# One ring of six slots, two longer output-weight loads, and 64 contraction rows of a modulation term by a second queue

## The chip, the core and the metric

The kernel runs on one core of a Trainium2 chip. The metric is the device time of one execution in microseconds. TensorE is PE in the profile, VectorE DVE, ScalarE ACT, GpSimd POOL, SyncE SP; SPq and ACTq are the queues on which those engines issue transfers.

## The reference

For a batch of 4 rows, one token each, width 512: six modulation rows come from a conditioning vector, grouped-query attention (32 query heads, 8 key/value heads, a cache of 4096 positions) is added to the residual with a gate, and a token-mixing MLP follows with its own shift, scale and gate. All is fp32.

```python
mod = (silu(c) @ w_mod).reshape(4, 6, 1, 512)          # w_mod: 512 x 3072
sa, ca, ga, sb, cb, gb = (mod[:, i] for i in range(6))
h = layernorm(x) * (1 + ca) + sa
q = (h @ wq)                                            # 512 x 4096
p = softmax(q k^T * 128**-0.5);  o = p v                # 32 caches of k and of v, 2 MB each
x = x + ga * (o @ wo)                                   # wo: 4096 x 512
h = layernorm(x) * (1 + cb) + sb
x = x + gb * (gelu(h * w1 + b1) @ w2 + b2)
```

The inputs weigh 157 MB, of which the key and value caches are 134 MB.

## The kernel before

There are 32 streams (4 batch rows x 8 key/value heads). Stream i has a key tile K[i] and a value tile V[i], each 128 partitions x 16 KB. All loads are issued by SyncE, in the order of the program, on one queue; SyncE waits at an instruction until the place that a load writes is free, and what stands behind it waits too. Below, K3V1 is the load of 4 MB that brings K[3] and V[1].

A pool `ring` holds three buffers of 2 x 16 KB a partition. They take first the modulation weights of terms 0 and 1 (`wm01`), and the two halves of `wq`, then `kk` (K0 and K1), then the pairs K2V0, K3V1, K4V2 and so on. The output weights have buffers of their own, four loads of 2 MB (`load_wo`). The modulation weights of terms 2, 3 and 4 (`wm24`, 3 MB in two loads) take one ring buffer for a while, and term 5 comes last of all.

The order of the instructions is that of the code: the schedule is manual. After the projection of the queries, iteration i of the main loop does for PE: `scores(i+2)` (L231), `pick(i-1)` (L328), `sums(i+1)`, `project(i-1)` (L343), `turn_max(i+2)`, the first half of `values(i)` (L291), `spread_max`, the second half of `values(i)`. So iteration 1 needs K3V1, and iteration 2 needs K4V2. In iteration 2 the three calls `mod(2)`, `mod(3)`, `mod(4)` follow: each multiplies silu(c), held by contraction block k = 0..3, with the four blocks of 128 rows of its weights (L215, tile `pm`), copies the result on ScalarE (L218) and folds the four groups (L221, tile `pc`), and a copy into `prep` frees the PSUM buffer for the next one. The last eight streams follow a written list of steps (`PLAN`), and after the last value tile comes a tail of vector and scalar work that ends in the stores.

Of the kernel before, what the change touches and what calls it, by code (L numbers as in the profile page):

```python
# [20 lines left out]
NSM = 3 * NF + 16 + 1  # L21
# [7 lines left out]
def adaln_decode(ctx: ExitStack, tc: tile.TileContext, small, x, wmod, wq, kk, kv, vv, wo, out):  # L29
# [18 lines left out]
    wm01 = ring.tile([P, 2, 4, D], F32, name="wm01", tag="kv")  # L48
    nc.sync.dma_start(wm01, wmod[0])
# [3 lines left out]
    for k in range(0, 4, 2):  # L53
        t = ring.tile([P, 2, HQ * DH], F32, name=f"wq{k}", tag="kv")
        nc.sync.dma_start(t, wq[k // 2])
        wqt += [t[:, 0], t[:, 1]]
    w1, b1, w2 = sm[:, 0:NF], sm[:, NF:2 * NF], sm[:, 2 * NF:3 * NF]
    cT = sm[:, 3 * NF:3 * NF + 16]
    b2 = sm[:, 3 * NF + 16:]
# [31 lines left out]
    wo_p = [wos.tile([P, 2, REP, D], F32, name=f"wo{h}") for h in range(0, HKV, 2)]  # L91
    wo_t = [wo_p[h // 2][:, h % 2] for h in range(HKV)]
    prep = cst.tile([P, 4, P], F32, name="prep")
    osb = cst.tile([P, B, P], F32, name="osb")
    sT8 = cst.tile([P, 4, B, 8], F32, name="sT8")

    def root(ve, n=P, y=None):
        if y is None:
# [4 lines left out]
    sg = cst.tile([P, 16], F32, name="sg")  # L103
# [3 lines left out]
    sT = cst.tile([P, 4, B], F32, name="sT")  # L107
    dv.tensor_mul(sT.rearrange("p k b -> p (k b)"), sg, cT)  # L108
    nc.gpsimd.tensor_copy(sT8.rearrange("p k b r -> p (k b) r"),
                   sT.rearrange("p k b -> p (k b)").unsqueeze(2).to_broadcast([P, 16, 8]))  # L110
# [46 lines left out]
    KT, VT, WM = {}, {}, {}  # L157

    def slots():
        return ring.tile([P, 2, SK], F32, name="kv", tag="kv")  # L160

    def key(t, i):
        KT[i] = t

    def value(t, i):
        VT[i] = t.rearrange("p (j d) -> p j d", d=DH)

    def load_first():
        t = slots()
        nc.sync.dma_start(t, kk)  # L170
        key(t[:, 0], 0)
        key(t[:, 1], 1)

    def load_pair(i):
        t = slots()
        nc.sync.dma_start(t, kv[i])
        key(t[:, 0], i + 2)
        value(t[:, 1], i)

    def load_wo(h):  # L180
        nc.sync.dma_start(wo_p[h // 2], wo[h // 2])

    def load_wm24():
        w = ring.tile([P, 3, 4, D], F32, name="wm24", tag="kv")
        nc.sync.dma_start(w[:, 0:2], wmod[1])
        nc.sync.dma_start(w[:, 2], wmod[2][:, 0])
        for e in range(3):
            WM[2 + e] = w[:, e]

    def load_wm5():  # L190
        t = slots().rearrange("p s (k n) -> p (s k) n", n=D)
        nc.sync.dma_start(t[:, 0:4], wmod[2][:, 1])
        WM[5] = t[:, 0:4]
        return t[:, 4:6]

    def load_key(t, i):
        nc.sync.dma_start(t, kv[i - 2][:, 0])
        key(t, i)

    def load_v(t, i, cuts):  # L200
        value(t, i)
        src = (kv[i][:, 1] if i < NS - 2 else vv[i - NS + 2]).rearrange("p (j d) -> p j d", d=DH)
        for lo, hi in zip(cuts, cuts[1:]):
            nc.sync.dma_start(VT[i][:, lo:hi], src[:, lo:hi])
# [7 lines left out]
    def mod(t):  # L212
        pm = ps_e.tile([P, D], F32, name=f"pm{t}", tag="e")
        for k in range(4):
            mm(pm[32 * k:32 * k + 32, :], sT8[:, k].rearrange("p b r -> p (b r)"), WM[t][:, k, :],  # L215
               start=True, stop=True)
        yw = wk.tile([P, D], F32, name="ym", tag="yw", bufs=1)
        nc.scalar.activation(yw, pm, AF.Copy)  # L218
        pc = ps_e.tile([P, P], F32, name=f"pc{t}", tag="e")
        for c in range(4):  # L220
            mm(pc[32 * c:32 * c + 32, :], g32, yw[:, c * P:(c + 1) * P], start=True, stop=True)  # L221
        return pc
# [3 lines left out]
    def scores(i):  # L226
        b, h = divmod(i, HKV)
        S[i] = s = ps_s.tile([P, 1024], F32, name=f"s{i}", tag="s")
        for n in range(2):
            for c in range(4):  # L230
                mm(s[32 * c:32 * c + 32, n * 512:(n + 1) * 512], QT[:, b, h, :],  # L231
                   KT[i][:, (n * 4 + c) * 512:(n * 4 + c + 1) * 512], start=True, stop=True)

# [51 lines left out]
    def values(i, ks):  # L285
        if ks[0] == 0:
            PV[i] = ps_v.tile([P, 4 * DH], F32, name="pv", tag="pv")
        pT = PL[i][0]
        for k in ks:
            q = k % 4  # L290
            mm(PV[i][32 * q:32 * q + 32, :], pT[:, 128 * k:128 * k + 128:4],  # L291
               VT[i][:, 4 * k:4 * k + 4, :].rearrange("p j d -> p (j d)"), start=(k < 4), stop=(k >= 4))

    def values_narrow(i, ks, pv=None):
        if ks[0] == 0:
            PV[i] = ps_v.tile([P, DH], F32, name="pvn", tag="pv") if pv is None else pv
        pv = PV[i]
        pT = PL[i][0].rearrange("p (k r) -> p k r", r=32)
        top = 32 if i < NS - 1 else 30
        for k in ks:  # L300
            for j in range(4 * k, min(4 * k + 4, top)):
                c = j % 4
                mm(pv[32 * c:32 * c + 32, :], pT[:, j, :], VT[i][:, j, :], start=(k == 0), stop=(j + 4 >= top))  # L303

# [32 lines left out]
    def project(i, pa=None, between=None):  # L337
        b, h = divmod(i, HKV)
        oT = OT[i]
        if pa is None:  # L340
            pa = ps_m.tile([P, D], F32, name="pa", tag="m")
            for g in range(REP):
                mm(pa[32 * g:32 * g + 32, :], oT[:, g:g + 1].to_broadcast([P, 32]), wo_t[h][:, g, :],  # L343
                   start=True, stop=True)
        else:
            for g in range(REP):
                for c in range(4):
                    mm(pa[32 * c:32 * c + 32, :], oT[:, g:g + 1].to_broadcast([P, 32]),  # L348
                       wo_t[h][:, g, c * P:(c + 1) * P], start=(g == 0 and h == HKV - 2),
                       stop=(g == REP - 1 and h == HKV - 1))  # L350
                if between and g == 1:
                    between()
        PA[i] = pa
# [198 lines left out]
    def finish(b, pg, py, hb, wr):  # L552
        uu = ring.tile([P, 16, D], F32, name="uu", tag="kv")
# [35 lines left out]
    def fold_gate(gate, es):  # L589
        for e in es:  # L590
            w = wo_t[HKV - 2 + e // REP][:, e % REP]
            dv.tensor_tensor_reduce(w, w, gate, 1.0, 0.0, OP.mult, OP.add, rowsum[:, e:e + 1])
# [16 lines left out]
    load_first()  # L609
    load_pair(0)  # L610
    load_wo(0)
    for i in range(2):
        for step in (scores, row_max, turn_max, col_max, spread_max, copy_max, expo):
            step(i)
    for step in (turn, sums, scale):
        step(0)
    mix = None
    for i in range(NS - HKV):
        load_pair(i + 1)
        if i in (1, 3, 5):  # L620
            load_wo(i + 1)
        if i == 1:
            load_wm24()
# [25 lines left out]
        if i == 2:  # L649
            for t in range(2, 5):  # L650
                pm = mod(t)
                dst = prep[:, {2: 1, 3: 2, 4: 3}[t]]
                if t == 4:
                    dv.tensor_scalar(dst, pm, 1.0, None, op0=OP.add)
                else:
                    nc.scalar.activation(dst, pm, AF.Copy)
        if i == NS - HKV - 2:
            gate = spread_gate()
# [4 lines left out]
    pve = pgx = pc = ep = spare = slot = None  # L663
    gates = list(range(2 * REP))
    cuts = {NS - 1: (0, 16, 24, 28, 30, 32), NS - 2: (0, 16, 32)}
    last, halves = [(0, 1, 2, 3), (4, 5), (6,), (7,)], [(0, 1), (2, 3), (4, 5), (6, 7)]
    PLAN = """
    a23 v24.0 A23 p23 t25.0 P23 F R v24.1 LP25 G s26 t25.1 M H V24 LP26 Q a24 S26 v25.0 N s27 x A24 f p24 g
    x LP27 m26 S27 P24 m27 X26 X27 b26 B26 e26 x b27 v25.1 c g t26.1 l25 t26.0 B27 s28 V25 c g L25
    v26.0 v26.1 S28 x l26 f a25 L26 V26 A25 x m28 p25 LT X28 e27 c a26 P25 t27.0 A26 b28 s29 f B28 p26 e28  # L670
    LK30 t27.1 S29 P26 v27.0 m29 l27 g LK31 T t28.1 X29 LT t28.0 s30 L27 S30 b29 v27.1 B29 e29 l28 m30 V27
    LV28 L28 a27 g X30 t29.1 t29.0 l29 L29 s31 A27 LV29 b30 p27 x B30 S31 c c m31 e30 P27 X31 v28.0 f LT LV30
    b31 v28.1 B31 f e31 LV31 l30 V28 L30 t30.1 l31 L31 a28 t31.1 A28 p28 v29.0 v29.1 t30.0 f P28 V29 v30.0 a29
    v30.1 A29 LW p29 f v30.2 v30.3 t31.0 P29 g V30 Y y a30 A30 p30 E x v31.0 f v31.1 v31.2 v31.3 V31 z31 a31 I A31 j p31
# [3 lines left out]
             "l": sums, "L": scale, "V": copy_v, "a": pick, "A": copy_o, "P": add_up,  # L678
             "LP": load_pair}
# [4 lines left out]
    for step in PLAN.split():  # L684
# [19 lines left out]
        elif op == "LT":  # L704
            slot = slots()
        elif op == "LK":
            load_key(slot[:, i % 2], i)
        elif op == "LV":
            load_v(slot[:, i % 2], i, cuts.get(i, (0, 32)))
        elif op == "LW":  # L710
            spare = load_wm5()
        elif op == "x":
            mix.expand(spare if mix.n == 6 else None)
# [75 lines left out]
```

## Time and profile before

| | |
|---|---|
| time, median of 3 runs | 386.42 us (386.37 to 386.49) |
| span of the profiled execution | 384.7 us |
| busy: PE, DVE, ACT, POOL | 298.7, 198.2, 112.2, 7.7 us |
| mean granted TensorE clock | 0.883 |
| read from HBM | 157.32 MB |

The page tells the span of the profiled execution, from its first to its last instruction; no separate time of that execution is given, and the median of the runs lies 1.7 us above the span. In the lines of the chain, a row has the start, the length and what the time went to; in a timeline, start, length, engine, source line, operation, tiles and count, and in brackets the idle time before it with what ended it. One matmul of the code is two records in the trace, so that x8 is four matmuls. A table of windows has for each window the busy time of each engine, the granted clock (1.00 is full speed), the busy share of the 16 DMA engines and GB/s.

### The profile page before, as it was taken

How to read it: one execution, taken by the hardware profiler on the slowest of the kernel's cores; microseconds unless marked ns; L12 is line 12 of the kernel's file. 1: busy time of each engine (PE TensorE's matmuls, PEld its weight loads, DVE VectorE, ACT ScalarE, POOL GpSimd, SP SyncE). 2: the span in 40 equal slices, each digit the busy share in tenths (PEclk: the TensorE clock that was granted, in tenths of full speed). 3: DMA queues.
4: the chain of work that ended last, by engine and by line, in shares of the span. 5: the costliest groups of instructions: out<-in, count | busy, mean ns of one | idle time of the engine just before them, and what ended most of it. 6: DMA issues, size and time to landing. Idle time of an engine off the chain costs nothing.

```text
span 384.7 us, 5604 instructions
## 1 busy us (share of the span) xinstructions
PE 298.7 (78%) x2380; PEld 117.2 (30%) x2380; DVE 198.2 (52%) x407; ACT 112.2 (29%) x144; POOL 7.7 (2%) x33
## 2 busy tenths in 40 slices
PE   0856777866966949979877878788888887999984
PEld 0112122311323313334322222342222343333653
DVE  1130251620451424664866545557665567778757
ACT  1001111121110110212567311124575105657276
POOL 1100000000000000000000000000000000000000
PEclk9989555985695685998999998999999999999999
DMA  8999999999999999999999999999999999999930
GB/s 331 433 433 436 411 453 433 409 432 436 423 441 433 434 436 436 434 436 431 429 425 433 428 433 434 429 433 431 429 434 436 434 436 432 424 417 423 418 122 3
DMA packets 7409, 157.69 MB, mean 410 GB/s; under 512 B 964, under 2 KB 1236, under 8 KB 1496
## 3 DMA queue, kind: packets, MB, share of 16 engines
q1 hardware_dynamic: 7376, 157.33, 95.4%
q8 instruction: 18, 0.29, 0.3%
q14 instruction: 7, 0.06, 0.0%
q10 hardware_dynamic: 8, 0.00, 0.0%
HBM read 157.32 MB, written 0.01 MB: 409 GB/s over the span
## 4 chain that ended last, share of the span: by engine, by line
DMA 60%; PE 29%; DVE 7%; ACT 2%; issue 1%; POOL 0%; SPq 0%; POOLq 0%; DVEq 0%
DMA kv<-in_kv 58%; PE s L231 8%; PE pv L291 7%; PE s L122 2%; PE qs L138 2%; DVE m L236 2%; DVE p L267 2%; DMA sm<-in_small 2%; PE pa L343 2%; PE pt L328 2%; ACT uu L562 1%; PE pb L251 1%; PE pve L303 1%; PE pm L240 1%; PE pgx L348 1%
## 5 line engine op out<-in xcount | busy, mean ns | idle before, releaser
L231 PE MATMUL s<-kv,QT 128*32 128x512 f32 x512 | 75.2, 714 | 38.9 <-DMA kv<-in_kv 37.0
L236 DVE TENSOR_REDUCE m<-s 128x1 f32<-128x1024 f32 x32 | 39.2, 1224 | 96.0 <-PE s L231 95.9
L261 ACT ACTIVATE p<-s,nm 128x1024 f32<-128x1024 f32 x32 | 35.7, 1115 | 180.6 <-DVE nm L256 180.5
L291 PE MATMUL pv<-kv,p 128*32 128x512 f32 x464 | 69.8, 670 | 0.7 <-DMA kv<-in_kv 0.7
L231 PEld LDWEIGHTS s<-kv,QT 128*32 128x32 f32 x512 | 15.8, 123 | 84.0 <-DMA kv<-in_kv 52.5
L328 PEld LDWEIGHTS pt<-g,po 128*128 128x128 f32 x236 | 31.1, 205 | 27.2 <-issue 19.9
L343 PE MATMUL pa<-wo,oT 128*32 128x512 f32 x240 | 34.6, 648 | 4.6 <-DVE oT L335 4.4
L328 PE MATMUL pt<-g,po 128*128 128x4 f32 (+2 forms) x236 | 33.9, 267 | 1.5 <-DVE po L314 1.0
L267 DVE STREAM_TRANSPOSE p<-p 128x1024 f32<-128x1024 f32 x25 | 30.9, 1234 | 0.0
L314 DVE COPY po<-pv 128x512 f32<-128x512 f32 x29 | 20.0, 688 | 16.8 <-PE pv L291 16.7
L245 DVE TENSOR_REDUCE mx<-pm 1x128 f32<-1x512 f32 x32 | 21.3, 669 | 1.1 <-PE pm L240 1.1
L442 DVE TENSOR_SCALAR u<-hb,wr,sm 128x512 f32<-128x512 f32 x40 | 19.9, 541 | 1.9 <-POOL wr L437 1.0
L506 ACT ACTIVATE u<-u 128x1024 f32<-128x1024 f32 x20 | 20.4, 1051 | 1.5 <-DVE u L442 1.4
L361 DVE TENSOR_TENSOR acc<-acc,pa 128x512 f32<-128x512 f32 x26 | 17.8, 686 | 4.3 <-PE pa L343 4.2
L261 ACT ACT_TABLE_LOAD x11 | 14.1, 1283 | 20.3 <-DVE nm L256 20.2
L251 PEld LDWEIGHTS pb<-neg,mx 1*128 1x128 f32 x64 | 10.4, 202 | 28.2 <-DVE mx L245 26.5
L122 PE MATMUL s<-wm,sT 128*4 128x512 f32 x16 | 9.1, 732 | 10.6 <-DVE sT L108 10.6
L506 ACT ACT_TABLE_LOAD x13 | 16.7, 1283 | 0.2
L291 PEld LDWEIGHTS pv<-kv,p 128*32 128x32 f32 x464 | 13.4, 146 | 7.2 <-issue 3.1
L240 PE MATMUL pm<-ident,m 128*1 128x128 f32 x32 | 9.3, 289 | 7.4 <-DVE m L236 3.5
L251 PE MATMUL pb<-neg,mx 1*128 1x1 f32 x64 | 13.1, 271 | 2.1 <-DVE mx L245 2.1
L453 PE MATMUL py<-u,sm 128*32 128x512 f32 x80 | 14.4, 616 | 0.0
(158 smaller groups left out, 214.7 us busy)
## 6 DMA issues: line engine op xcount, KB each, us to landing
kv<-in_kv SPq DMA_DIRECT2D x28, 4096.0 KB, 21.9
wq<-in_wq SPq DMA_DIRECT2D x2, 4096.0 KB, 16.3
wo<-in_wo SPq DMA_DIRECT2D x4, 2048.0 KB
kv<-in_kv SPq DMA_DIRECT2D x4, 2048.0 KB, 20.3
wm<-in_wmod SPq DMA_DIRECT2D x2, 2048.0 KB, 14.8
kv<-in_kk SPq DMA_DIRECT2D x1, 4096.0 KB
kv<-in_vv SPq DMA_DIRECT2D x3, 1024.0 KB
wm<-in_wmod SPq DMA_DIRECT2D x1, 1024.0 KB
```

Of the source, the lines that this page charges most:

```text
L231: mm(s[32 * c:32 * c + 32, n * 512:(n + 1) * 512], QT[:, b, h, :], KT[i][:, (n * 4 + c) * 512:(n * 4 + c + 1) * 512], start=True, stop=True)
L236: dv.tensor_reduce(M[i], S[i], axis=AX.X, op=OP.max)
L245: dv.tensor_reduce(mx, M[i].rearrange("o (c r) -> o r c", c=4).unsqueeze(1).to_broadcast([1, 4, 32, 4]), axis=AX.X, op=OP.max)
L251: mm(pb, M[i].rearrange("o c r -> o (c r)"), neg1, start=True, stop=True)
L261: nc.scalar.activation(p, S[i], AF.Exp, bias=M.pop(i), accum_out=l)
L267: dv.transpose(PL[i][0], PL[i][0])
L291: mm(PV[i][32 * q:32 * q + 32, :], pT[:, 128 * k:128 * k + 128:4], VT[i][:, 4 * k:4 * k + 4, :].rearrange("p j d -> p (j d)"), start=(k < ...
L314: dv.tensor_copy(PV[i], pv)
L328: mm(pt, po[:, c * DH:(c + 1) * DH], sel.unsqueeze(1).to_broadcast([P, m, REP]), start=(c == 0), stop=(c == n - 1))
L343: mm(pa[32 * g:32 * g + 32, :], oT[:, g:g + 1].to_broadcast([P, 32]), wo_t[h][:, g, :], start=True, stop=True)
L442: dv.tensor_scalar(u[:, e, :], hb, wr[:, j:j + 1], b1[:, j:j + 1], op0=OP.mult, op1=OP.add)
L506: nc.scalar.activation(u, u, AF.Gelu_apprx_tanh)
```

## The change

- The pool of three buffers becomes one tile `RING` of six slots of 16 KB a partition. A list `LOADS` holds all loads in the order in which they are issued, and `advance(name)` is called after the last reader of a tile in the code; it issues the loads at the head of the list as far as the slots that they take have been read, and stops at the first that has to be held back.
- `wm01` no longer takes ring space. It is loaded into the place of output weights 0 and 1; `kk` so takes the free slots 4 and 5 at once.
- The output weights come in two loads of 4 MB in place of four of 2 MB. The first goes behind K2V0. The second takes the place in which the weights of terms 2, 3 and 4 lie in the meantime (`wm24` and `low`, inside output weights 4 to 7), so that it is held until `mod(4)` has read them (`advance("M2")`). It stands in the list behind K4V2 and ahead of K5V3.
- The weights of terms 2, 3 and 4 are loaded behind K3V1, 22 KB a partition in one load, and half a block (`wm24[0:64, 11]`) in another. The three `mod` calls move from the end of iteration 2 to the end of iteration 1.
- The last 64 contraction rows of term 3 are brought by ScalarE's queue, in two loads of 8 rows of 8 KB, to 16 of 64 partitions of `low`, which GpSimd sets to zero before. The matching rows of silu(c) come as extra columns of `small`, zeros elsewhere; `mod(3)` uses one matmul over 64 partitions and four more over `low` in place of its fourth.
- In the last eight streams, loads go by slot in place of by pairs of slots.

```diff
-    ring = ctx.enter_context(tc.tile_pool(name="ring", bufs=3))
+    ring = ctx.enter_context(tc.tile_pool(name="ring", bufs=1))
...
-    wm01 = ring.tile([P, 2, 4, D], F32, name="wm01", tag="kv")
-    nc.sync.dma_start(wm01, wmod[0])
+    RING = ring.tile([P, 6, SK], F32, name="kv")
+    wo_t = wos.tile([P, HKV, REP, D], F32, name="wo")
+    wm01 = wo_t[:, 0:2]
+    wm24 = wo_t[:, 4:7].rearrange("p h g n -> p (h g) n")
+    low = wo_t[0:64, 7]
+    nc.sync.dma_start(wm01, wm0)
...
+    nc.gpsimd.memset(low, 0.0)
...
+    def queue():
+        q = [entry(["K0", "K1"], kk)]
+        for i in range(NS - 4):
+            q.append(entry([f"K{i + 2}", f"V{i}"], kv[i]))
...
+        q.insert(2, ("wo", "M0", wo_t[:, 0:4], wo[0]))
+        q.insert(4, ("wo", None, wm24[:, 0:11], wm2))
+        q.insert(5, ("wo", None, wm24[0:64, 11], wm3))
+        q.insert(7, ("wo", "M2", wo_t[:, 4:8], wo[1]))
+        return q
...
+    def advance(name=None):
+        read.add(name)
+        while LOADS:
+            kind, names, *rest = LOADS[0]
+            if kind == "wo":
+                if names not in read:
+                    return
+                nc.sync.dma_start(*rest)
+            else:
+                n, p = len(names), at[0]
+                if any(h not in read for h in held[p:p + n]):
+                    return
...
     def mod(t):
...
-            mm(pm[32 * k:32 * k + 32, :], sT8[:, k].rearrange("p b r -> p (b r)"), WM[t][:, k, :],
-               start=True, stop=True)
+            if t == 3 and k == 3:
+                mm(pm[96:128, :], sT8[0:64, 3].rearrange("p b r -> p (b r)"), wm24[0:64, 11], start=True, stop=False)
+                for q in range(4):
+                    mm(pm[96:128, :], sT8[0:64, 4 + q].rearrange("p b r -> p (b r)"), low[:, q],
+                       start=False, stop=(q == 3))
+            else:
+                mm(pm[32 * k:32 * k + 32, :], sT8[:, k].rearrange("p b r -> p (b r)"), WM[t][:, k, :],
+                   start=True, stop=True)
...
     for i in range(2):
         for step in (scores, row_max, turn_max, col_max, spread_max, copy_max, expo):
             step(i)
+        nc.scalar.dma_start(low[i:64:8].rearrange("p g n -> p (g n)"), wlow[i])
...
     for i in range(NS - HKV):
-        load_pair(i + 1)
-        if i in (1, 3, 5):
-            load_wo(i + 1)
-        if i == 1:
-            load_wm24()
         scores(i + 2)
...
-        if i == 2:
+        if i == 1:
             for t in range(2, 5):
                 pm = mod(t)
...
+            advance("M2")
```

SyncE's queue, from the first key load to the seventh pair, before. `wo` is a load of output weights, `wm` the modulation weights of terms 2 to 4, `kv` a pair, and 128x8192 fp32 elements are 4 MB.

```order
L170 DMA kv<-in_kk 128x8192
L176 DMA kv<-in_kv 128x8192
L181 DMA wo_128<-in_wo 128x4096
L176 DMA kv<-in_kv 128x8192 x2
L181 DMA wo_129<-in_wo 128x4096
L185 DMA wm_337<-in_wmod 128x4096
L186 DMA wm_337<-in_wmod 128x2048
L176 DMA kv<-in_kv 128x8192 x2
```

The same stretch of SyncE's queue in the changed kernel.

```order
L208 DMA kv<-in_kk 128x8192
L208 DMA kv<-in_kv 128x8192
L190 DMA wo<-in_wo 128x8192
L208 DMA kv<-in_kv 128x8192
L190 DMA wo<-in_wm 128x5632
L190 DMA wo<-in_wm 64x512
L208 DMA kv<-in_kv 128x8192
L190 DMA wo<-in_wo 128x8192
L208 DMA kv<-in_kv 128x8192 x25
```

The first `wo` now has twice the bytes and stands ahead of K3V1 as before; the `wm` loads moved from behind K4V2 to ahead of it; and the second `wo` (which waits for `mod(4)`) stands between K4V2 and the 25 pairs from K5V3 on.

TensorE from the scores of iteration 2 through the modulation terms, before (`s` scores, `pt` pick, `pa` project, `pv` values, `pm_445` to `pc_478` the three `mod` calls).

```order
L231 MATMUL s_394<-kv,QT 32x512 x8
L328 MATMUL pt<-g_122,po 128x4 x4
L275 MATMUL pl<-g_122,l 128x4
L343 MATMUL pa<-wo_128,oT 32x512 x4
L240 MATMUL pm<-ident,m 1x128
L291 MATMUL pv<-kv,p 32x512 x4
...
L215 MATMUL pm_445<-wm_337,sT_134 32x512 x4
L221 MATMUL pc_452<-ym,g_122 32x128 x4
L215 MATMUL pm_458<-wm_337,sT_134 32x512 x4
L221 MATMUL pc_465<-ym,g_122 32x128 x4
L215 MATMUL pm_471<-wm_337,sT_134 32x512 x4
L221 MATMUL pc_478<-ym,g_122 32x128 x4
```

TensorE in the changed kernel, from the scores of iteration 1 (`s_332`, which read K3) to those of iteration 2 (`s_430`).

```order
L249 MATMUL s_332<-kv,QT 32x512 x8
...
L366 MATMUL pa<-wo,oT 32x512 x4
...
L310 MATMUL pv<-kv,p 32x512 x4
L233 MATMUL pm_384<-wo,sT_129 32x512 x4
L239 MATMUL pc_391<-ym,g_121 32x128 x4
L233 MATMUL pm_397<-wo,sT_129 32x512 x3
L228 MATMUL pm_397<-wo,sT_129 32x512
L230 MATMUL pm_397<-wo,sT_129 32x512 x4
L239 MATMUL pc_408<-ym,g_121 32x128 x4
L233 MATMUL pm_414<-wo,sT_129 32x512 x4
L239 MATMUL pc_421<-ym,g_121 32x128 x4
L249 MATMUL s_430<-kv,QT 32x512 x8
```

The three terms now stand one iteration earlier, ahead of the scores of iteration 2, and the middle one has eight matmuls in place of four.

More of the change, by code (lines that the diff above doesn't have):

```diff
@@ L180, in load_wo @@
[L180 to L204, printed above, removed]
+    KT, VT, WM = {}, {}, {t: wm24[:, k:k + 4] for t, k in ((2, 0), (3, 4), (4, 7))}
+    held, read = [("Q", 0), ("Q", 0), ("Q", 1), ("Q", 1), None, None], {None, ("Q", 0), ("Q", 1)}
@@ new lines, in adaln_decode, with entry @@
+    cuts = {NS - 1: (0, 16, 24, 28, 30, 32), NS - 2: (0, 16, 32)}
+    def entry(names, src):
+        return ("ring", names, src)
+    def queue():
+        q = [entry(["K0", "K1"], kk)]
+        for i in range(NS - 4):
+            q.append(entry([f"K{i + 2}", f"V{i}"], kv[i]))
+        for i in (NS - 2, NS - 1):
+            q.append(entry([f"K{i}"], kv[i - 2][:, 0]))
+        for i in range(NS - 4, NS):
+            q.append(entry([f"V{i}"], kv[i][:, 1] if i < NS - 2 else vv[i - NS + 2]))
+        q.append(entry(["W5"], wm5))
+        q.insert(2, ("wo", "M0", wo_t[:, 0:4], wo[0]))
[3 more added lines that the diff above has]
+        return q
@@ new lines, in adaln_decode @@
+    LOADS, at = queue(), [4]
+    def advance(name=None):
[10 more added lines that the diff above has]
+                    return
+                for k, nm in enumerate(names):
+                    t, i = RING[:, p + k], int(nm[1:])
+                    if nm[0] == "K":
+                        KT[i] = t
+                    elif nm[0] == "V":
+                        VT[i] = t.rearrange("p (j d) -> p j d", d=DH)
+                    else:
+                        WM[i] = t.rearrange("p (k n) -> p k n", n=D)[:, 0:4]
+                held[p:p + n] = names
+                at[0] = (p + n) % 6
+                if names[0] == "W5":
+                    nc.sync.dma_start(WM[5], rest[0])
+                elif len(names) > 1:
+                    nc.sync.dma_start(RING[:, p:p + n], rest[0])
+                elif names[0][0] == "K":
+                    nc.sync.dma_start(RING[:, p], rest[0])
+                else:
+                    cs = cuts.get(i, (0, 32))
+                    v = rest[0].rearrange("p (j d) -> p j d", d=DH)
+                    for lo, hi in zip(cs, cs[1:]):
+                        nc.sync.dma_start(VT[i][:, lo:hi], v[:, lo:hi])
+            LOADS.pop(0)
@@ L348, in project @@
                     mm(pa[32 * c:32 * c + 32, :], oT[:, g:g + 1].to_broadcast([P, 32]),
-                       wo_t[h][:, g, c * P:(c + 1) * P], start=(g == 0 and h == HKV - 2),
+                       wo_t[:, h, g, c * P:(c + 1) * P], start=(g == 0 and h == HKV - 2),
                        stop=(g == REP - 1 and h == HKV - 1))
@@ L764 @@
     cT = a["c"].reshape(B, 4, P).transpose(2, 1, 0).reshape(P, 16)
+    low = _np.zeros((P, 16), _np.float32)
+    low[0:64].reshape(8, 8, 4, B)[:, 0:2] = a["c"][:, 448:].reshape(B, 8, 2, 4).transpose(1, 2, 3, 0)
+    cT = _np.concatenate([cT, low], axis=1)
     small = _np.concatenate([
```

95 lines of the change are left out of this document (37 added, 58 removed).

## The prediction

> **What bounds the kernel now.** I read the page first (busy time, the DMA lines, the chain's shares), then the chain in order of time, SyncE's queue in the timeline, and last the windows.
>
> ```profile
> span 384.7 us, 5604 instructions
> PE 298.7 (78%) x2380; PEld 117.2 (30%) x2380; DVE 198.2 (52%) x407; ACT 112.2 (29%) x144; POOL 7.7 (2%) x33
> GB/s 331 433 433 436 411 453 433 409 432 436 423 441 433 434 436 436 434 436 431 429 425 433 428 433 434 429 433 431 429 434 436 434 436 432 424 417 423 418 122 3
> q1 hardware_dynamic: 7376, 157.33, 95.4%
> DMA 60%; PE 29%; DVE 7%; ACT 2%; issue 1%; POOL 0%; SPq 0%; POOLq 0%; DVEq 0%
> kv<-in_kv SPq DMA_DIRECT2D x28, 4096.0 KB, 21.9
> ...
> 0.00:2.00 2.00, 0.00 (x0) 0.00 (x0) 0.49 (x2) 1.28 (x1) 0.71 (x7) 1.00 0.56 106
> 0.00:5.00 5.00, 0.00 (x0) 0.00 (x0) 1.42 (x3) 1.28 (x1) 0.71 (x7) 1.00 0.65 206
> 2.00:82.00 80.00, 52.84 (x283) 15.64 (x283) 24.27 (x49) 7.93 (x18) 2.31 (x15) 0.81 0.99 425
> 83.30:362.00 278.70, 229.14 (x1735) 90.57 (x1735) 158.28 (x315) 90.20 (x109) 3.96 (x9) 0.90 1.00 431
> ```
>
> The loads are the bound: from 2 to 362 us the DMA engines are 99 to 100% busy, at 433 GB/s in most slices. A pair of 4.19 MB takes 4.19/0.433 = 9.7 us, but 21.9 us from issue to landing: some 12 us of other loads lie ahead of it when it is issued. As long as that reserve is above zero, waits of SyncE cost nothing. Once it is used up, every microsecond without a load comes back at the end, since the same bytes are still to come:
>
> ```profile
> 63.14 3.30 PE s L231 x16
> ...
> 71.80 22.74 DMA kv<-in_kv
> 94.58 3.64 PE s L231 x16
> ...
> 327.22 15.81 DMA kv<-in_kv
> 343.04 0.14 issue
> ```
>
> The chain runs on loads up to 343.04 us, where K30 has come, and what follows goes with the last tiles. So I ask of each part whether it takes DMA time away, and whether it lets the queue run dry.
>
> **Parts that cost nothing, or little.** `kk` is issued some 17 us sooner, behind loads that are busy anyway (share 0.99 above): 0. The finer releases of the last tiles: 0, by the same reserve. Longer rows of the output weights, 32 KB against 16 KB: the slices in which most tiles of the end are loaded by half (424, 417 and 423, from the 35th on) against those of whole pairs (425 to 436) are slower by 3% at the most, and 8.4 MB take 19 us, so between 0 and -0.6 us; those slices hold still shorter pieces too, so I take -0.1. The 64 rows: 128 KB come by another queue. Spread evenly nothing changes. If an 8-row load runs on 8 of the 16 engines, those carry 16 KB more and all carry 8 KB less; at 433/16 = 27 GB/s an engine that is 0.3 us more or less on the half that ends last, so -0.3 to +0.3, taken 0. ("How many engines" in the Trainium skill's DMA: Bandwidth & Descriptors, section "Why a DMA increments its semaphore by 16 and not by 1", has such a load on the lowest-numbered 8; by it the sum would shift by one of these two ends, and no view here names the engines.)
>
> The zeros for `low` stand on POOL ahead of the sigmoid from which the whole start follows:
>
> ```profile
> 0.74 0.20 POOL masks.py:197 MEMSET ident<- 128x128 f32 x1
> 9.72 0.10 POOL L81 MEMSET eps<- 128x1 f32 x1
> ...
> 50.76 1.11 ACT L261 ACTIVATE p<-s,nm 128x1024 f32<-128x1024 f32 x1 [5.44 <-DVE nm L256]
> ...
> 35.64 0.42 PE L153 MATMUL px<-xr,rows 4*32 4x128 f32 x8
> 37.90 2.94 PE L231 MATMUL s<-kv,QT 128*32 128x512 f32 x16 [1.84 <-DMA kv<-in_kk]
> ...
> 30.10 0.33 SPq L176 DMA_DIRECT2D kv<-in_kv  x1
> 33.53 14.31 SPq L176 DMA_DIRECT2D kv<-in_kv  x2
> ```
>
> 0.10 us for 127 more elements makes 1.6 us for 2048 (an estimate). The query projection is that much later; PE's wait of 1.84 us for `kk` hides it, and the issue of K2V0, at 31.7 in place of 30.10, still comes with `kk` in flight (landing near 37). 0. Without that cover it would be 1.6 us of PE in iteration 0, which has the next wait to spend. The two issues on ACT (0.33 us each, as SP's) fall into its idle time beside the first exponentials (5.44 us before the second): 0.
>
> **The part that costs: the second output-weight load.** It waits for the last matmul of `mod(4)`, and K5V3 and all that follows is queued behind it on SyncE, though K5V3's slots are free long before. Four times decide.
>
> *When the queue runs dry.* Ahead of it stand wm01 2.10, small and x 0.04, wq 8.39, kk, K2V0, K3V1 and K4V2 4.19 each, the first output weights 4.19, the terms 3.15: 34.6 MB, the same bytes as before. The windows moved 0.21 MB to 2 us and 425 x 80 = 34.0 MB to 82 us; the other 0.43 MB make 83.0, and since a packet counts where it starts, I take 83.2. From the other side: K5V3, issued at 71.80 with the queue full, is there for PE at 94.58, less 9.7 is 84.9, which holds the slowest engine and the signal. 83.2 is nearer to the mean over the engines.
>
> *When iteration 1 starts.* K3V1 now has 2.10 MB more ahead of it, 4.84 us: 63.14 + 4.84 = 67.98.
>
> *How long it takes, and the terms behind it.*
>
> ```profile
> 62.60:65.90 3.30, 2.76 (x16) 0.59 (x16) 0.00 (x0) 0.00 (x0) 0.00 (x0) 0.50 0.87 377
> 66.00:83.00 17.00, 12.70 (x102) 4.88 (x98) 9.21 (x16) 2.41 (x4) 0.00 (x0) 1.00 1.00 427
> 83.10:103.50 20.40, 15.63 (x91) 4.32 (x83) 4.01 (x7) 2.35 (x5) 0.00 (x0) 0.50 0.98 424
> 141.20:154.60 13.40, 11.35 (x53) 4.15 (x57) 4.04 (x7) 0.63 (x1) 0.00 (x0) 0.50 1.01 435
> 155.00:160.00 5.00, 4.63 (x43) 2.00 (x39) 3.70 (x6) 0.17 (x2) 0.00 (x0) 1.00 0.97 416
> ...
> 63.14 3.30 PE L231 MATMUL s<-kv,QT 128*32 128x512 f32 x16 [2.54 <-DMA kv<-in_kv]
> 70.64 1.09 PE L291 MATMUL pv<-kv,p 128*32 128x512 f32 x8
> 72.81 1.92 PE L231 MATMUL s<-kv,QT 128*32 128x512 f32 x16 [1.08 <-DMA kv<-in_kv]
> 78.92 1.09 PE L291 MATMUL pv<-kv,p 128*32 128x512 f32 x8
> ...
> 143.25 3.64 PE L231 MATMUL s<-kv,QT 128*32 128x512 f32 x16 [5.20 <-DMA kv<-in_kv]
> 153.61 1.59 PE L291 MATMUL pv<-kv,p 128*32 128x512 f32 x8
> ...
> 82.51 1.47 PE L215 MATMUL pm<-wm,sT 128*32 128x512 f32 x8 [2.49 <-DMA wm<-in_wmod]
> 84.67 0.66 PE L221 MATMUL pc<-ym,g 128*32 128x128 f32 x8 [0.70 <-ACT ym L218]
> 85.73 1.94 PE L215 MATMUL pm<-wm,sT 128*32 128x512 f32 x8 [0.40 <-ACT prep L656]
> 88.44 0.66 PE L221 MATMUL pc<-ym,g 128*32 128x128 f32 x8 [0.78 <-ACT ym L218]
> ```
>
> An iteration depends on the granted clock. After a wait of 2.54 us, iteration 1 of before got the full clock from 66.0 and took 63.14 to 71.73, 8.6 us. One that starts after 5.20 us of waiting stayed at half clock for 13.4 us: 143.25 to 155.20, 11.95 us. One wholly at full clock took 72.81 to 80.01, 7.2 us. In the changed kernel PE waits for K3V1 from 60.6 to 67.98, 7.4 us, and the changes of clock lie on a grid of 3.41 us (66.0 to 83.0 is five, 83.1 to 103.5 six): the scores of before filled the window 62.6 to 65.9 to 2.76 of 3.30 us, and it rose. From 67.98 they would straddle 69.4, 1.4 us and 2.2 us, as those at 143.25 did. I take 11.95: iteration 1 ends at 79.9.
>
> The terms at full clock: pm 1.09 (as `pv`, the same shape), 0.70 for the copy, pc 0.4 (as `px`, 128 columns at full clock), 0.40 for the second copy, 2.6 us; `mod(3)` with twice the matmuls 2.18 + 1.5 = 3.7; pm of `mod(4)` 1.09; together 7.4 us. At half clock: 3.8 + (3.88 + 1.84) + 1.94 = 11.4. Since the iteration that began at 143.25 had the full clock by 155, some 11.5 us after its start, this one has it from about 79.5, and I take 7.4: the last read is at 87.3. The weights are there by then: they follow K3V1 by 3.15 MB, 7.3 us.
>
> *How long until data flows.* The first load is issued at 0.72 and 206 x 5 = 1.03 MB have gone by 5.0 us, which at 433 GB/s began at 2.62: 1.9 us after the issue.
>
> ```profile
> 0.72 0.39 SPq L49 DMA_DIRECT2D wm<-in_wmod  x1
> ```
>
> So the stream resumes at 89.2 where it ended at 83.2: 6.0 us without loads. Nothing later gives them back: after it the wo load, K5V3 and K6V4 stand in the queue at once (29 us), while iteration 2 (some 88 to 100) frees the slots of K7V5. The terms leave iteration 2, but there they lay in PE's wait for K5V3 (81 to 94.5 us): no gain.
>
> **The sum**, on the profiled execution: 384.7 + 6.0 - 0.1 = 390.6, and with the 1.7 us around it 392.3; on the median 386.4 + 5.9 = 392.3.
>
> **Rivals.**
>
> *Iteration 1 gets the full clock early.* Then it ends at 67.98 + 8.6 = 76.6, the last read is at 84.0, data at 85.9, 2.7 us dry: 389.0. For it: the scores are dense, 3.6 us at half clock, and fill one window if it starts near them. Against it: the longer wait, and the grid as it lay in this execution. The Trainium skill's TensorE: Matmul & The Clock Gate ("What's actually happening") calls the window of 4096 cycles free-running, not reset by the kernel's start; the 3.41 us grid agrees, and by that rule the phase could be another in each run.
>
> *The terms stay at half clock.* 79.9 + 11.4 = 91.3, data at 93.2, 10 us dry: 396.4. For it: all three ran so at 83 to 92 us, with gaps for the copies. Against it: the window ahead of them is full of `pv`.
>
> *The queue does not run dry (not slower).* The second wo load has to be issued ahead of 83.2 - 1.9 = 81.3. With the fastest rows, 67.98 + 7.2 + 7.4 = 82.6, it misses that by 1.3 us; it decides if K3V1 comes sooner, or a warm queue takes a new load in less than 1.9 us. Then only the rest of the sum is left: 386.4 - 0.1, with the balance of the engines at best -0.4: 386.0 to 386.6. A gain above 0.2% would need both of those ends and something I don't see.
>
> **How the numbers follow.** Half-clock iteration with full-clock terms, as summed, 0.47 (390.7 to 394, its ends being the dry time 84.9 and part of the terms at half clock); full clock early 0.27; terms at half clock 0.12; never dry 0.10, of which nearly all ends within 0.2% (0.8 us; the runs before lay within 0.12 us of each other); faster by another way 0.04. The likeliest gives 392.3. The range, 388.4 to 396.5, takes in the first three cases with half of the third's spread. Slower 0.87, same 0.09, faster 0.04.
>
> **What would show it.** In the slices of the page, GB/s falls to some 300 in the ninth and tenth (77 to 96 us), where it was 432 and 436; on SyncE a wait of its wo issue on PE `pm` L233, with the issue near 87; PE `s` of iteration 1 at 68 with a DMA wait of about 7 us; the later slices as before, and the chain's end later by the hole. If the hole is missing and the time still rises, the start (POOL's zeros) or the tail is at fault. The prediction fails if the clock is granted sooner at 68 to 80 us, or if a queue that has just emptied restarts faster than at the kernel's start.

## The result, and the profile after

The changed kernel takes 395.78 us (median of 5 runs, 395.02 to 396.04) against 386.49 us before (5 runs, 386.37 to 387.85): a ratio of 1.0233, 95% interval 1.0219 to 1.0247, so 9.3 us slower where 5.9 were predicted. The profiled execution took 395.8 us with a span of 394.0, which is 9.3 us over the span of before.

The page after has the hole where it was forecast, deeper than forecast. Rows: span; busy time; GB/s in 40 slices of 9.85 us; the queue of the 8-row loads, with packets and MB; the chain's shares.

```profile
span 394.0 us, 5617 instructions
PE 294.9 (75%) x2388; PEld 116.7 (30%) x2388; DVE 198.4 (50%) x407; ACT 112.2 (28%) x144; POOL 9.6 (2%) x34
GB/s 327 429 429 452 394 419 427 404 238 314 426 427 426 434 442 436 434 429 427 426 428 439 437 433 431 432 429 424 432 431 449 427 434 427 422 423 428 415 118 4
q10 hardware_dynamic: 40, 0.13, 0.1%
DMA 59%; PE 30%; DVE 6%; ACT 2%; issue 1%; POOL 1%; SPq 0%; POOLq 0%; DVEq 0%; ACTq 0%
```

POOL is busy for 9.6 us in place of 7.7, the zeros. The ninth and tenth slices moved 238 and 314 GB/s. The fifth and eighth, 394 and 404, are a little lower than those of before (411 and 409, in slices of 9.62 us): around the two 8-row loads, which ScalarE issues near 43 and 47 us, and the half block. Slices that begin at other times compare only roughly. Windows of the same microseconds (length; PE, PEld, DVE, ACT, POOL busy; granted clock; DMA share; GB/s) make this sharper. After:

```profile
44.00:56.00 12.00, 7.61 (x36) 2.08 (x32) 6.29 (x9) 1.20 (x2) 0.00 (x0) 0.64 1.03 410
72.00:77.00 5.00, 5.00 (x27) 2.71 (x27) 3.08 (x5) 0.00 (x0) 0.00 (x0) 0.50 1.02 363
77.00:84.00 7.00, 5.89 (x43) 1.35 (x36) 1.66 (x4) 2.08 (x4) 0.00 (x0) 0.93 1.01 433
84.00:92.20 8.20, 6.28 (x45) 1.66 (x47) 0.29 (x1) 1.47 (x3) 0.00 (x0) 1.00 0.28 88
92.20:362.00 269.80, 215.73 (x1599) 84.56 (x1588) 155.18 (x301) 84.47 (x101) 3.95 (x9) 0.92 1.00 431
```

Two of the same windows of before:

```profile
44.00:56.00 12.00, 9.06 (x40) 2.62 (x35) 4.67 (x8) 2.41 (x4) 0.00 (x0) 0.50 1.01 434
72.00:77.00 5.00, 3.98 (x34) 1.76 (x34) 2.69 (x4) 0.21 (x2) 0.00 (x0) 1.00 1.02 433
```

So there are two losses. From 84 to 92.2 us the queue is nearly empty (share 0.28), and at 44 to 56 and 72 to 77 us the engines are fully busy (1.03 and 1.02) but move only 410 and 363 GB/s. From 92.2 to the end the rate is as before, and nothing comes back.

The chain after, in order of time (start, length, what), and SyncE's timeline and wait:

```profile
35.28 33.40 DMA kv<-in_kv
...
79.70 0.90 PE pm L233 x8
...
84.13 3.45 PE pm L230 x8
...
89.13 1.11 PE pm L233 x8
90.29 0.33 SPq L190
90.62 0.05 issue
90.67 22.20 DMA kv<-in_kv
```

```profile
90.29 0.33 SPq L190 DMA_DIRECT2D wo<-in_wo  x1
90.67 234.52 SPq L208 DMA_DIRECT2D kv<-in_kv  x25
...
SPq L190 <- PE pm L233: 13.4, 1, 13.4
```

In front of the second output-weight load SyncE first waits 32.0 us for the weights of the terms to land, and then 13.4 us for the last `pm` of `mod(4)`, which reads them; all 25 pairs stand behind it. The three terms in TensorE's timeline:

```profile
68.73 3.64 PE L249 MATMUL s<-kv,QT 128*32 128x512 f32 x16 [10.67 <-DMA kv<-in_kv]
...
82.10 1.06 PE L233 MATMUL pm<-wo,sT 128*32 128x512 f32 x6 [0.40 <-ACT prep L673]
83.09 1.04 PE L228 MATMUL pm<-wo,sT 64*32 64x512 f32 x2
83.97 3.59 PE L230 MATMUL pm<-wo,sT 64*32 64x512 f32 x8
89.13 1.06 PE L233 MATMUL pm<-wo,sT 128*32 128x512 f32 x8 [0.40 <-ACT prep L673]
```

Eight records of `pm` take 1.06 us when they go to four groups of 32 columns (the last row), and the four matmuls over `low` take 3.59 us at the same full clock: all four write `pm[96:128]`, one group, and run one behind another.

### The profile page after: what moved, and what is told of

It reads as the page before. It is cut to its first block, busy times and chain, and to the rows that moved or that the text cites. A ratio compares the mean times of both kernels' runs of the same rounds, so it can differ in the third digit from the quotient of the medians.

```text
span 394.0 us, 5617 instructions
## 1 busy us (share of the span) xinstructions
PE 294.9 (75%) x2388; PEld 116.7 (30%) x2388; DVE 198.4 (50%) x407; ACT 112.2 (28%) x144; POOL 9.6 (2%) x34
## 4 chain that ended last, share of the span: by engine, by line
DMA 59%; PE 30%; DVE 6%; ACT 2%; issue 1%; POOL 1%; SPq 0%; POOLq 0%; DVEq 0%; ACTq 0%
DMA kv<-in_kv 57%; PE s L249 7%; PE pv L310 6%; PE s L124 2%; PE qs L140 2%; DMA sm<-in_small 2%; DVE p L286 2%; DVE m L255 2%; PE pt L351 2%; PE pa L366 2%; ACT kv L585 1%; PE pve L324 1%; PE pb L270 1%; PE pm L230 1%; PE pm L233 1%
## 5 line engine op out<-in xcount | busy, mean ns | idle before, releaser
L249 PE MATMUL s<-kv,QT 128*32 128x512 f32 x512 | 72.9, 694 | 53.0 <-DMA kv<-in_kv 53.0
L310 PE MATMUL pv<-kv,p 128*32 128x512 f32 x464 | 67.7, 651 | 0.7 <-DMA kv<-in_kv 0.6
L366 PE MATMUL pa<-wo,oT 128*32 128x512 f32 x240 | 34.6, 648 | 4.4 <-DVE oT L358 4.2
L124 PE MATMUL s<-wo,sT 128*4 128x512 f32 x16 | 9.1, 732 | 12.3 <-DVE sT L110 12.3
L270 PEld LDWEIGHTS pb<-neg,mx 1*128 1x128 f32 x64 | 9.6, 188 | 27.6 <-DVE mx L264 25.9
```

The lines of the kernel that those rows point to most:

```text
L270: mm(pb, M[i].rearrange("o c r -> o (c r)"), neg1, start=True, stop=True)
```

## The experiments

Theory A: the hole is the loss. Theory B, the rival: the short loads slow the stream. A third question was whether the granted clock in iteration 1 sets the hole's length. Medians are of the runs given, and ratios are to runs of before taken together with them (medians 386.45 to 386.47 us). A time in a trace is that of one run.

**The second output-weight load one place later** (behind K5V3; nothing else changed).

```diff
-        q.insert(7, ("wo", "M2", wo_t[:, 4:8], wo[1]))
+        q.insert(8, ("wo", "M2", wo_t[:, 4:8], wo[1]))
```

> The changed kernel with the second output-weight load one place further back in the list, behind K5V3 in place of ahead of it. Theory (the hole in the load stream, 7.2 us from 85.0 to 92.2, is the loss): K5V3 covers 9.7 us, so the loads no longer stop; left are the 1.7 us by which the stream was already late at 85 us: 388.0 us (387.3 to 388.7). Rival (the ring's other order, the zeros at the start or the tail cost the time): it stays above 394.

388.59 us (10 runs, 387.77 to 389.86), ratio 1.0041, interval 1.0011 to 1.0071: inside the expected band. Its window:

```profile
84.00:92.00 8.00, 6.08 (x44) 1.59 (x46) 0.29 (x1) 1.47 (x3) 0.00 (x0) 1.00 1.01 434
```

The hole is gone, and with it 395.78 - 388.59 = 7.2 us of 9.3. SyncE still waits for `mod(4)` (its issue is at 89.89), but a pair is in flight meanwhile. Some 2 us stay.

**No short loads**: terms 2 to 4 come whole in one load, without `low`, its zeros and its matmuls. Once with the second output-weight load in its old place, once behind K5V3.

```diff
-        q.insert(4, ("wo", None, wm24[:, 0:11], wm2))
-        q.insert(5, ("wo", None, wm24[0:64, 11], wm3))
-        q.insert(7, ("wo", "M2", wo_t[:, 4:8], wo[1]))
+        q.insert(4, ("wo", None, wm24[:, 0:12], wm2))
+        q.insert(6, ("wo", "M2", wo_t[:, 4:8], wo[1]))   # second kernel: 7
```

> The changed kernel without the separate way of the 64 rows: the terms 2 to 4 come in one load of 24 KB a partition on SyncE's queue, no zeros, no loads from ScalarE, four matmuls in mod(3). The second output-weight load stays ahead of K5V3. Theory: the stream is 1.7 us earlier at its dry point (83.2), iteration 1 starts 1.2 us earlier, the terms are 3.3 us shorter, so the last read is near 85.0 to 85.8, loads flow again at 86.9 to 87.7: a hole of 3.7 to 4.5 us, 390 to 391 us. Rival (the 64 rows have no part in it, all is the place of the load): 394 or more.

> Both: terms 2 to 4 in one load, and the second output-weight load behind K5V3. Theory: no hole and no slow small loads, so the time before less what longer rows bring: 386.3 us (385.9 to 386.6). Rival (the small loads cost nothing by themselves): the same time as with the load further back alone.

The first took 390.52 us (10 runs, 388.1 to 391.96; 1.0088, 1.0055 to 1.0121), the second 386.56 (10 runs, of which nine lie from 386.5 to 386.75 and one at 391.31; 1.0002, 0.9966 to 1.0038). Both are as expected. In the second kernel's windows the two slow stretches are gone:

```profile
44.00:56.00 12.00, 7.84 (x37) 2.40 (x34) 6.29 (x9) 1.21 (x2) 0.00 (x0) 0.62 1.01 437
72.00:77.00 5.00, 4.63 (x40) 1.66 (x39) 3.63 (x8) 1.14 (x2) 0.00 (x0) 1.00 1.06 457
```

With neither hole nor short loads, the changed order, the ring of six and the longer rows neither cost nor bring anything that these runs can tell, which is 0.4% by the interval.

**The four matmuls of `low` in four column groups**, so that they run beside each other.

```diff
-                    mm(pm[96:128, :], sT8[0:64, 4 + q].rearrange("p b r -> p (b r)"), low[:, q],
-                       start=False, stop=(q == 3))
+                    mm(pm[32 * q:32 * q + 32, :], sT8[0:64, 4 + q].rearrange("p b r -> p (b r)"), low[:, q],
+                       start=False, stop=True)
```

> The changed kernel with the four extra matmuls of mod(3) each in a column group of its own (the four groups are summed by the fold behind them anyway) in place of all in the last group. Theory (in one group they follow each other at 0.43 us a record, in four they overlap as the others do, 0.136 a record): mod(3) is 3.3 us shorter less what the overlap leaves, the hole shrinks by 2.4 to 3.3, 392.4 to 393.4 us. Rival (a matmul over 64 rows is slow by itself): unchanged within 0.5 us, 395.8.

396.14 us (4 runs, 393.19 to 396.63), ratio 1.0207, 1.0133 to 1.028. The median missed the expectation. The profiled run, 393.19, does show the shorter term, in TensorE's timeline:

```profile
70.40 3.56 PE L249 MATMUL s<-kv,QT 128*32 128x512 f32 x16 [11.16 <-DMA kv<-in_kv]
...
81.65 1.06 PE L233 MATMUL pm<-wo,sT 128*32 128x512 f32 x6 [0.40 <-ACT prep L673]
82.64 0.61 PE L228 MATMUL pm<-wo,sT 64*32 64x512 f32 x1
82.64 0.63 PE L230 MATMUL pm<-wo,sT 64*32 64x512 f32 x3
83.09 0.59 PE L228 MATMUL pm<-wo,sT 64*32 64x512 f32 x1
83.09 1.44 PE L230 MATMUL pm<-wo,sT 64*32 64x512 f32 x5
```

From 81.65 to 84.5 it is 2.9 us where the changed kernel needed 5.5, and the output-weight load was issued at 87.27. But the other three runs were no faster than the changed kernel, and the profiled run differs from it in more than the groups: its iteration 1 started 1.7 us later and took 8.9 us (70.40 to 79.25) in place of 11.0, since the full clock came sooner. So the term is shown to be shorter; that the time of the other runs was lost by the clock is a guess, as they have no trace. The next kernels were meant to take the clock out of it:

**TensorE kept busy ahead of iteration 1** by matmuls on K2 that nothing reads: 24 of them; then 36; then 36 together with the four groups.

```diff
+        if i == 1:
+            warm = ps_e.tile([P, D], F32, name="warm", tag="e")
+            for r in range(9):        # 6 in the first kernel
+                for c in range(4):
+                    mm(warm[32 * c:32 * c + 32, :], QT[:, 0, 0, :], KT[2][:, c * 512:(c + 1) * 512],
+                       start=True, stop=True)
```

> The changed kernel with 24 matmuls whose results nobody reads, put in front of the scores of iteration 1, into PE's wait for K3V1. Theory (iteration 1 is 11 us long because PE has waited 11 us and is granted half the clock): the full clock holds through the scores, iteration 1 takes 7.2 to 8 us from about 68.5, the last read of mod(4) moves from 90.2 to some 87, the hole from 7.2 to 4 us: 392 to 393 us. Rival (the clock plays no part, the iteration waits for something else): 395.8 us, unchanged.

395.31 us (4 runs, 393.92 to 396.47; 1.0204, 1.0149 to 1.026), not told from the changed kernel. In its trace the filler ended 5.3 us before K3V1 came, and the scores ran at half clock (3.64 us). Iteration 1 was shorter all the same, 8.9 us, but the clock fell again in the terms (the last `pm` took 1.94 us), and the output-weight load was issued at 89.58, hardly sooner than at 90.29.

> The changed kernel with 36 unread matmuls in PE's wait for K3V1 (24 ended 5 us ahead of it, and the clock fell again). Theory (the clock decides iteration 1): the scores of iteration 1 run at full clock, iteration 1 takes 7.2 us, the last read of mod(4) is near 87, the hole 4 us: 392 to 393 us, with less spread than the changed kernel's. Rival (the clock plays no part): 395.8.

> The same 36 unread matmuls, and the four extra matmuls of mod(3) in a column group each. Theory (one column group makes them follow each other): with the clock held, mod(3) is 2.6 us shorter, so is the hole: 2.6 us below the run with the 36 matmuls alone, 389.5 to 390.5. Rival: the same time as that run.

The longer filler alone took 395.54 us (4 runs, 393.7 to 397.82; 1.0223, 1.0173 to 1.0273), and missed. With the four groups it took 391.6 (4 runs, 390.19 to 393.99; 1.013, 1.0073 to 1.0186), 1.1 us over its expected band, and 3.9 below the filler alone where 2.6 were expected. TensorE's timelines, first of the filler alone, then with the groups:

```profile
56.41 7.91 PE L645 MATMUL warm<-kv,QT 128*32 128x512 f32 x72
68.99 3.44 PE L249 MATMUL s<-kv,QT 128*32 128x512 f32 x16 [4.68 <-DMA kv<-in_kv]
...
87.15 1.07 PE L233 MATMUL pm<-wo,sT 128*32 128x512 f32 x8 [0.40 <-ACT prep L679]
```

```profile
58.47 8.98 PE L645 MATMUL warm<-kv,QT 128*32 128x512 f32 x72
69.04 1.92 PE L249 MATMUL s<-kv,QT 128*32 128x512 f32 x16 [1.58 <-DMA kv<-in_kv]
...
83.75 1.07 PE L233 MATMUL pm<-wo,sT 128*32 128x512 f32 x8 [0.40 <-ACT prep L679]
```

The same filler ended at 64.32 in one run and at 67.45 in the other: the work before it and the filler itself ran at another clock. So the filler did not fix the clock of the scores, and the two kernels differ in it too: iteration 1 took 8.7 and 7.2 us. What the groups alone did is read from the term: the matmuls of `mod(3)` took 5.5 us in the first trace and 2.9 in the second, the 2.6 us expected. Where the scores began at full clock (1.92 us), iteration 1 ended 7.2 us after its start, and the second output-weight load was issued at 84.91, about when the queue ran dry; 1.7 us of hole were left. On the third question the traces agree with each other: with an iteration 1 of 11.0 us the hole was 7.2 us, with 8.7 us it was 5.4. The medians of the two fillers alone don't show it.

The miss of the longer filler has a second part, which is not explained. Its loads ran 2.0 us ahead of those of the changed kernel (K29V27 landed at 343.13 in place of 345.12, mean over the DMA engines, from the packet records), yet its span is only 0.3 us shorter. Its chain no longer runs through loads to the end; its shares, and the window in which TensorE fell back to half clock:

```profile
DMA 46%; PE 37%; DVE 10%; ACT 4%; POOL 1%; issue 1%; SPq 0%; POOLq 0%; ACTq 0%; DVEq 0%
...
298.00:312.00 14.00, 13.17 (x77) 5.16 (x73) 5.78 (x10) 1.99 (x4) 0.00 (x0) 0.66 1.01 435
```

In that window the changed kernel had clock 1.00. This fits engines that lie close behind the loads, so that a late fall of the clock takes away what the stream has won. It is not shown: no run changed that window alone, and the four groups without a filler have a chain with as little DMA (42%), though their time follows the loads within 0.8 us.

**The two 8-row loads on SyncE's queue**, behind the half block, with the second output-weight load behind K5V3.

```diff
-        q.insert(7, ("wo", "M2", wo_t[:, 4:8], wo[1]))
+        for i in range(2):
+            q.insert(6 + i, ("wo", None, low[i:64:8].rearrange("p g n -> p (g n)"), wlow[i]))
+        q.insert(10, ("wo", "M2", wo_t[:, 4:8], wo[1]))
...
-        nc.scalar.dma_start(low[i:64:8].rearrange("p g n -> p (g n)"), wlow[i])
```

> The output-weight load further back (no hole), and the two 8-row loads issued by SyncE behind the half block in place of ScalarE. Theory A (a second queue beside the full one costs the 0.8 us seen at 44 to 56 us): 387.8 us, against 388.6 with ScalarE's queue. Theory B (a short load costs the same on any queue): 388.6 us or above.

388.08 us (12 runs, 387.31 to 392.38; 1.0047, 1.002 to 1.0074). The median lies between the two theories, and the intervals don't tell it from 388.59. Its windows settle more:

```profile
44.00:56.00 12.00, 9.07 (x42) 2.77 (x34) 6.29 (x9) 1.28 (x3) 0.00 (x0) 0.50 1.01 434
72.00:77.00 5.00, 4.63 (x40) 1.53 (x39) 3.63 (x8) 1.16 (x2) 0.00 (x0) 1.00 1.08 317
```

The stretch from 44 to 56 us is whole again, and the one in which the 8-row loads now lie fell to 317 GB/s, from 377 in the kernel with only the half block there. So the loss went with the loads. In the packet records the stream is 1.5 us late with either queue; the other 0.5 us between the medians is not explained.

**The last block of the terms in two loads of 64 partitions** of 2 KB, without `low`, the second output-weight load behind K5V3.

```diff
+        q.insert(4, ("wo", None, wm24[:, 0:11], wm2[:, 0:11]))
+        q.insert(5, ("wo", None, wm24[0:64, 11], wm2[0:64, 11]))
+        q.insert(6, ("wo", None, wm24[64:128, 11], wm2[64:128, 11]))
+        q.insert(9, ("wo", "M2", wo_t[:, 4:8], wo[1]))
```

> The output-weight load further back, no separate way for the 64 rows, but the last block of the terms in two loads of 64 partitions x 2 KB in place of being part of the long load. Theory B (short loads cost by themselves, 0.9 us for the one half block at 73 to 76 us): 386.5 + 1 to 1.8, 387.5 to 388.3 us. Theory A (only the second queue costs): 386.6 us, as without the split.

387.19 us (12 runs, 386.94 to 388.65; 1.0014, 0.9994 to 1.0035), 0.6 us over the kernel with the whole block: small, and inside the interval of that ratio. It lies between the two theories; the packet records have the stream 0.5 us late, half of what Theory B asked at least.

To see such loads by themselves, one pair in the middle of the kernel before (K16V14, 4 MB) was cut: into 112, 8 and 8 rows, and into two of 64.

```diff
-        nc.sync.dma_start(t, kv[i])
+        if i == 14:
+            for lo, hi in ((0, 112), (112, 120), (120, 128)):   # second kernel: ((0, 64), (64, 128))
+                nc.sync.dma_start(t[lo:hi], kv[i][lo:hi])
+        else:
+            nc.sync.dma_start(t, kv[i])
```

> The kernel before with one pair (K16 and V14) in three loads: 112 rows, 8 rows and 8 rows of 32 KB. If an 8-row load runs on one half of the 16 engines and the 18 instruction packets of 16 KB all fall on the other half, which then ends some 3 us behind, this takes one row of 1.2 us off the late half: 385.3 to 386.0 us. Rival (short loads cost about 0.5 us each, or the late engines are others): 386.5 to 388 us.

> The kernel before with one pair (K16 and V14) in two loads of 64 partitions x 32 KB in place of one of 128, the same bytes and row length. Theory (16 engines that write 64 partitions share their write paths two by two, as the 112-row load went at half the rate): each half goes at some 217 GB/s, 9.7 us more in all, less what lies over by the neighbours: 391 to 396 us. Rival (only loads of fewer than 16 rows, or a count of rows that is not a power of two, are slow): 386.4 to 387.

403.08 us (6 runs, 401.82 to 404.05; 1.0416, 1.0378 to 1.0455) and 398.81 us (4 runs, 397.77 to 399.97; 1.0305, 1.0268 to 1.0343). The first had been meant to balance the engines, and failed by 17 us; the second came out 2.8 us over its band. Windows of before, of the 64-row halves, and of the 112, 8 and 8 rows:

```profile
200.00:225.00 25.00, 19.82 (x164) 7.59 (x164) 15.09 (x27) 12.05 (x14) 0.00 (x0) 1.00 1.00 432
```

```profile
203.00:222.00 19.00, 10.66 (x61) 3.89 (x61) 6.63 (x12) 8.58 (x9) 0.00 (x0) 0.71 0.99 216
```

```profile
200.00:210.00 10.00, 7.14 (x39) 2.91 (x35) 3.75 (x8) 5.65 (x6) 0.00 (x0) 0.70 1.02 256
216.00:224.00 8.00, 0.00 (x0) 0.00 (x0) 0.00 (x0) 1.86 (x2) 0.00 (x0) 0.60 1.01 115
224.00:226.00 2.00, 0.00 (x0) 0.00 (x0) 0.00 (x0) 0.00 (x0) 0.00 (x0) 0.50 0.29 66
```

But for the last window, the 16 DMA engines count as busy in all of them. A load of 64 partitions moves at 216 GB/s, half of 432, one of 112 rows at 256, and loads of 8 rows at 115, about a quarter: each packet takes longer (with 64 partitions 2.45 us for 32 KB, the median, against 1.21). With 64 partitions the 4.19 MB need 4.19/0.216 = 19.4 us in place of 9.7, +9.7 of the 12.3 measured. The packet records have that stream 11.5 us late by 225 us and no later at its end, so nearly all of the cost lies in the two loads and at their edges. In the kernel with three loads it is 15.6 us late by 229 us; a part of that is the last window, in which the engines stood still most of the time (share 0.29), so these 17 us are not the price of the short loads alone.

## Why the prediction was right or wrong

The direction, the place and the mechanism held, and the time lies in the range; the size of two terms did not. That the range took the time in is partly luck: 395.78 lies above the ends of the likeliest case (390.7 to 394), in the part that the range owes to the rival of half-clock terms (396.4), and that rival did not happen. The terms ran at full clock and were long for another reason. The packet records give each kernel's books. A load has landed, here, at the mean over the 16 engines of the end of its last packet. "Late" is the landing of the same first 34.6 MB against before (83.27 us). The hole is what the next 4.19 MB took beyond 9.69 us.

| kernel | late | hole | sum | profiled run against before |
|---|---|---|---|---|
| changed | 1.7 | 7.2 | 8.9 | +9.3 |
| second `wo` load later | 1.5 | 0.0 | 1.5 | +1.8 |
| whole block | -0.1 | 1.4 | 1.3 | +1.6 |
| whole block, `wo` later | -0.1 | 0.0 | -0.1 | +0.1 |
| four groups | 1.9 | 4.0 | 5.9 | +6.7 |
| four groups, 36 fillers | 1.8 | 1.7 | 3.5 | +4.8 |
| 24 fillers | 1.2 | 7.0 | 8.2 | +10.0 |
| 36 fillers | 1.6 | 5.4 | 7.0 | +9.0 |
| half blocks, `wo` later | 0.5 | 0.0 | 0.5 | +0.5 |
| 8-row loads by SyncE, `wo` later | 1.5 | 0.0 | 1.5 | +2.3 |

The sum comes within 0.8 us of each time, except in the kernels with fillers (1.3 to 2.0 us), where the rest is not explained.

By the prediction's steps:

- *Start of iteration 1*, 67.98: 68.73. The 0.75 is the late stream: without the short loads the scores began at 67.83 and 67.94. PE had waited 10.67 us, not 7.4, as it was through with iteration 0 sooner than before.
- *Its length*, 11.95 at half clock: 68.73 to 79.70, 11.0 us. Held, within 1 us.
- *The terms*, 7.4 us: 79.70 to 90.24, 10.5. **This step failed**, in one summand. I counted `mod(3)` as twice the matmuls, 2.18 us, with all copies 3.7; its matmuls took from 82.10 to 87.56, 5.5 us, and with the copies 7.0, since the four of `low` share one column group. `mod(2)` took 2.4 for 2.6 and the last `pm` 1.1 as predicted. The rows of before that I used, `pv` and `pm`, all spread over four groups, and I didn't look at the addresses of the new ones. The Trainium skill bears on it (TensorE: Matmul & The Clock Gate, "Measured speedup vs the span model"): three column tiles of N=512 ran 2.38 times as fast as one after another. The trace agrees in kind: 3.59 us for eight records in one group, 1.06 in four.
- *When data flows again*, 1.9 us after the issue: issue at 90.29, full flow from about 92.2. Held: an emptied queue restarts as at the kernel's start.
- *When it runs dry*, 83.2: at 84.95, because the stream was 1.7 us late. This shortens the hole by as much as the stream is late, so that the two cancel: the time follows from when data flows again.
- *The 64 rows*, taken 0 within 0.3: **the second step that failed**, though it moved this kernel's time only by the later start of iteration 1; it shows in full once the hole is gone. I spread their bytes over the engines and took the rate of one engine as given. At the rates of the cut pair, 0.13 MB in a 64-row load takes 0.6 us in place of 0.3 and 0.13 MB in 8-row loads 1.1 in place of 0.3: +1.1 us, an estimate from those windows. Measured were 1.5 (loads on SyncE's queue) and 2.0 (on ScalarE's), each as the medians' distance to 386.56. What makes the rest is open.
- *Longer rows*, -0.1: the whole block with the later `wo` load equals before, so not told from 0.
- *POOL's zeros*, 1.6 us behind a cover: 1.80 us, and the scores of iteration 0 began at 37.78 (before 37.90). Covered. The two issues on ACT took 1.17 and 0.58 us, where 0.33 each were counted; no wait behind them shows. The rows, of POOL and of PE:

```profile
9.61 1.80 POOL L97 MEMSET wo<- 64x2048 f32 x1
...
37.78 1.92 PE L249 MATMUL s<-kv,QT 128*32 128x512 f32 x16
```

So data flowed again 3.0 us later than forecast: +0.75 by the start of iteration 1, -0.95 by its length, +3.1 by the terms, the rest rounding. The predicted 6.0 became 7.2 of hole and 1.7 of late stream, 8.9 together. The time grew by 0.4 us more; the packet records have the stream 8.9 us late from the hole to its end, so this lies behind the last loads, and was not traced.

The rivals: the early full clock is real. In the kernel with the whole block iteration 1 took 8.7 us, close to the 8.6 that this rival was given, and the last read was at 82.6:

```profile
67.83 3.36 PE L242 MATMUL s<-kv,QT 128*32 128x512 f32 x16 [9.44 <-DMA kv<-in_kv]
...
81.55 1.06 PE L226 MATMUL pm<-wo,sT 128*32 128x512 f32 x8 [0.40 <-ACT prep L665]
```

In the changed kernel's profile it did not occur. The whole-block kernel's runs spread from 388.1 to 391.96 us. I know no other cause for that than the clock's phase; it would fit the Trainium skill's rule of a free-running window that the prediction named, but no run fixed the phase, so it is not shown. "Never dry" happens when the order is changed, as the later `wo` load shows.

## What to carry to other kernels

In a kernel bound by one stream of loads, a load that must wait for a reader belongs behind as many other loads as fill that wait: moving one entry of the list by one place was worth 7.2 us here. Keep loads at 128 partitions, and price a load of fewer from a window of its rate, not from its bytes. When matmuls are added, look at which column group each writes before their duration is taken from a row of matmuls that spread.

## What the runs showed of the hardware that I had not expected

- A load of 64 partitions with 32 KB rows ran at 216 GB/s, one of 112 rows at 256 and two of 8 rows at 115, with the engines' share at 0.99, 1.02 and 1.01, against 432 for 128 partitions. One 4 MB pair cut in halves cost 12.3 us of a 386 us kernel. The Trainium skill's DMA: Bandwidth & Descriptors ("Rules for kernel authors") advises against two transfers to partition halves because they serialize; the trace agrees with the advice, but its cost is more than serialization, since at the measured rate the two halves together take twice the time of the whole. The same page ("The descriptor swizzle") gives each of 16 engines one port of its own in a transfer of 128 partitions; half the rate for half the partitions would follow if engines shared ports, which no run here shows directly.
- Loads of 8 rows cost the stream of 128-partition loads beside them: over 12 us, with 131 KB in those loads, it was 410 GB/s in the changed kernel and 422 with the later `wo` load, against 434 before and 437 with the whole block.
- Four matmuls over 64 rows in one column group took 3.59 us, four over 128 rows in four groups 1.06 us, at the same clock. Spread over four groups, the five matmuls over 64 rows took 1.9 us (82.64 to 84.53) in place of 4.5 (83.09 to 87.56).
